# Fused attention and gated MLP: heads 0 to 7 of the output projection move into the MLP pass, weight splits move behind q and k, and twelve row maxima move into the prologue

## Chip, cores and metric

The kernel runs on one core of a Trainium2 chip. The metric is device time in microseconds (us) for one execution. Of the kernel before, three timed runs gave a median of 1876.55 us (1875.42 to 1880.77). One more execution was taken by the hardware profiler; every row quoted below is from that one.

## The reference, cut to what is computed

```
xn = layernorm(x)                       # x: 2048 x 512
q, k, v = xn @ wqkv                     # 32 heads of 16
attention = softmax(q k^T / 4) v, heads side by side, @ wo
z  = gelu(xn @ w_in)                    # 2048 x 1792
z1 = z[:, :896];  z2 = layernorm(z[:, 896:])
g  = w_sp @ z2 + b_sp                   # mixes the 2048 rows
out = x + attention + (z1 * g) @ w_out
```

All inputs are float32. The output is 2048 x 512.

## The kernel before: how the work is laid out

The kernel body runs once, as Python, and emits a fixed list of instructions for each engine. It has two parts: a **prologue** (lines 1005 to 1048) whose order is that of the code, and a **main loop** (lines 1264 to 1302) in which a small planner chooses the next TensorE (PE) instruction at each step. The planner keeps an estimated clock for each engine (`T`) and books its own cost for each operation. Nothing of it runs on the chip. On the chip each engine executes its list in order and waits on semaphores where data or buffers are not ready.

Precise products are made of three matmuls of parts ("hi" and "lo" halves of a float32, `split`, `mm3`, `dense`). A weight is split on GpSimd (POOL): a copy (L286) and a subtraction (L288), in `weight`. A split weight can be stored to DRAM (`ahead_of_time`) and fetched again later without POOL (`fetch_parts`).

**Attention** is done for 16 pairs of heads. For each pair and each of four chunks of 512 queries the loop makes:

- 16 *maxima* slots (`maxima`, L1128): two matmuls (L1136) into one PSUM slot and one VectorE (DVE) reduction of 128 x 1024 (L839 in `max_red`). After the 16th, `max_fin` reduces and transposes the result, stores it (`mscr`), and two DMAs from `mscr` write the maximum into the last rows of `qst`.
- 16 *score* slots (`scores`, L1122): two matmuls into a PSUM slot and one ScalarE (ACT) exponential (L74). A chunk's scores may start only when `maxready` says that its row has arrived. Before the first score the loop makes maxima only (from planner time `FIRST` = 7 on, up to `LEAD` = 30 of them) and dense slots.
- two *value* bursts (`values`, L1219): 32 matmuls each. There are 128 bursts, and the text calls the stretch from one burst to the next a **round**. `ORDER` lists a round's slots: S scores, M maxima, D dense, V the burst.

The PSUM slots are three tiles `sl` and one tile `dps` of two banks each. In the main loop `dps` belongs to the **dense** slots (L1181): two matmuls that run side by side on the upper and the lower 64 rows of the array. The dense work is a queue of generators (L1059): v of the later rows, q and k of the later heads, the z2 half of the MLP, its z1 half, the spatial mix, the MLP's output product (`mlp_out`), the attention's output product (`attn_out`). A generator yields slots in *pieces* of about 24 (`"q"` ends a piece) and evacuates `dps` at the end of an accumulation (`"e"`). After a piece ends, `hold` keeps the next one back until the next burst. So the queue advances one piece in a round. When no dense slot can be had, `filler` (L1195) may issue two dummy matmuls.

Buffers of 512 KB (`piece`, a ring of 19) are counted in `room["big"]`; generators and loaders wait on this count, and 256 KB buffers `t512` (4) are counted in `room["t5"]`.

Places that the change touches:

- Prologue: for each group g of 512 rows, `qk_first(g)` makes q and k of the first heads, `load_stacks` brings them into `qst` and `kst` through DRAM, `turn_x` and `norm_x` prepare the next group, and `v_tile` makes the first four v tiles. Their accumulators are taken in turn from (`dps`, `sl0`, `sl1`, `sl2`) by `bank()`.
- L1053: seven z1 weight splits (`w1`) are started at the head of the main loop. `wsp`, the 16 weights of the spatial mix's first 512 columns, are split at L631, when z1's last but one piece begins.
- `z2_all` (L557): before its last piece it waits until `room["big"] > 5`, and fetches group 0 of the normalized input for z1. `z1_all` follows.
- `spatial` (L681): waits until all four `t512` are free (L685), loads two z1 tiles, and then works through 28 units of 48 slots, two pieces each.
- `norm_out` (L863): normalizes the attention output of eight heads of one chunk: two POOL products, a split and a store to `oscr`. It waits for the one `ogrp` buffer.
- `mlp_out` (L777): 16 pieces of 21 slots (7 blocks of `w_out`, three matmul pairs each). `attn_out` (L926): 8 pieces of 24 slots (4 blocks of `wo`), each followed by the addition `fin` (L929); it waits for the heads of the last group but one (`lasthl`). The last pair of heads is added at the end by `last_pair` (L962), `last_norm`, `last_mm` (L977) and `last_add` (L984), which wait for the `fin` additions.

## Time and profile before

| what | value |
|---|---|
| timed runs, median | 1876.55 us |
| the profiled execution, its own time | 1873.65 us |
| its span, first to last instruction | 1871.9 us |
| mean granted TensorE clock | 0.994 |
| first dense slot of the main loop | 64.07 us |
| first score matmul | 105.20 us |
| first value burst, last value burst (start) | 119.2 us, 1845.1 us |
| GpSimd busy | 721.0 us (39%) |
| ScalarE busy | 1188.7 us (64%) |

The span is one execution seen by the profiler; what lies around it is 1.75 us. Its own time is 2.9 us below the median of the timed runs, so a sum made against the profile is carried over to the median as a difference. In rows of a timeline the columns are start, duration, engine, line, operation, output<-inputs, form and count; a bracket gives the idle time before and what ended it. In rows of a table by windows, each pair is busy time and count.

### The profile page before, as it was taken

How to read it: one execution, taken by the hardware profiler on the slowest of the kernel's cores; microseconds unless marked ns; L12 is line 12 of the kernel's file. 1: busy time of each engine (PE TensorE's matmuls, PEld its weight loads, DVE VectorE, ACT ScalarE, POOL GpSimd, SP SyncE). 2: the span in 40 equal slices, each digit the busy share in tenths (PEclk: the TensorE clock that was granted, in tenths of full speed). 3: DMA queues.
4: the chain of work that ended last, by engine and by line, in shares of the span. 5: the costliest groups of instructions: out<-in, count | busy, mean ns of one | idle time of the engine just before them, and what ended most of it. 6: DMA issues, size and time to landing. Idle time of an engine off the chain costs nothing.

```text
span 1871.9 us, 38101 instructions
## 1 busy us (share of the span) xinstructions
PE 1821.7 (97%) x14848; PEld 1103.6 (59%) x14848; DVE 1443.5 (77%) x1677; ACT 1188.7 (64%) x1292; POOL 721.0 (39%) x808
## 2 busy tenths in 40 slices
PE   6989999999999999999999999999999999999998
PEld 5756566655654565466666656565655656555555
DVE  6568878888897887878787878777877878788863
ACT  2147777687676677766666666566656666666653
POOL 5412242778879768710145203400352222002110
PEclk9999999999999999999999999999999999999999
DMA  7836572533566343366568665744766757475544
GB/s 230 295 121 190 193 238 87 126 91 109 135 225 192 117 125 98 88 152 150 153 196 194 175 170 164 177 129 128 186 189 163 185 155 181 119 150 158 154 132 142
DMA packets 209309, 297.75 MB, mean 159 GB/s; under 512 B 36049, under 2 KB 107281, under 8 KB 206241
## 3 DMA queue, kind: packets, MB, share of 16 engines
q1 hardware_dynamic: 200008, 265.44, 51.8%
q0 software_dynamic: 9120, 29.89, 4.9%
q8 instruction: 116, 1.90, 0.4%
q14 instruction: 65, 0.52, 0.1%
HBM read 189.60 MB, written 105.65 MB: 158 GB/s over the span
## 4 chain that ended last, share of the span: by engine, by line
PE 85%; DVE 5%; POOL 4%; issue 2%; DMA 2%; ACT 1%; SPq 0%; DVEq 0%; POOLq 0%; ACTq 0%
PE dps L1181 33%; PE sl L1219 23%; PE sl L1122 14%; PE sl L1136 12%; DVE mm L839 4%; PE dps L1195 1%; POOL wsp L288 1%; ACT pf L74 1%; POOL wsp L286 1%; DMA zs<-z2scr 0%; PE sl L242 0%; PE sl L241 0%; PE sl L240 0%; POOL z2hl L542 0%; DMA kscr<-qkhl 0%
## 5 line engine op out<-in xcount | busy, mean ns | idle before, releaser
L839 DVE TENSOR_REDUCE mm<-sl 128x2 f32<-128x1024 f32 x1024 | 1224.2, 1222 | 209.2 <-PE sl L1136 204.7
L74 ACT ACTIVATE pf<-sl 128x1024 f32<-128x1024 f32 x1024 | 1041.1, 1026 | 337.3 <-PE sl L1122 300.1
L1219 PE MATMUL sl<-pf,vall 128*32 128x512 f32 x4096 | 467.3, 597 | 0.0
L1122 PE MATMUL sl<-qst,kst 50*128 50x512 f32 x2048 | 443.3, 422 | 14.0 <-DVE mm L839 5.1
L1181 PE MATMUL dps<-wsp,zs 64*128 64x512 f32 x2688 | 439.4, 393 | 2.7 <-DMA zs<-z2scr 2.7
L1136 PE MATMUL sl<-kst,qst 48*128 48x512 f32 x2048 | 427.1, 407 | 3.4 <-DVE mm L839 1.8
L1122 PEld LDWEIGHTS sl<-qst,kst 50*128 50x128 f32 x2048 | 197.7, 184 | 225.5 <-issue 84.0
L1181 PEld LDWEIGHTS dps<-wsp,zs 64*128 64x128 f32 x2688 | 265.0, 187 | 44.8 <-DMA zs<-z2scr 4.7
L1219 PEld LDWEIGHTS sl<-pf,vall 128*32 128x32 f32 x4096 | 120.3, 110 | 268.3 <-issue 236.1
L1136 PEld LDWEIGHTS sl<-kst,qst 48*128 48x128 f32 x2048 | 198.1, 185 | 109.6 <-ACT pf L74 57.6
L747 POOL TENSOR_TENSOR hhl<-z1i,hhl 128x512 fp32r<-128x512 f32 x28 | 35.6, 1284 | 371.4 <-ACT hhl L74 371.4
L74 ACT ACTIVATE e<-sl 128x512 f32<-128x512 f32 x64 | 38.2, 598 | 212.6 <-PE sl L1219 194.2
L1239 DVE TENSOR_TENSOR e<-sl,e 128x512 f32<-128x512 f32 x64 | 44.3, 692 | 132.3 <-PE sl L1219 68.9
L1181 PE MATMUL dps<-w,xt 64*128 64x448 f32 x768 | 110.8, 368 | 1.5
L1181 PE MATMUL dps<-wout,hp 64*128 64x512 f32 x672 | 109.6, 392 | 0.0
L882 POOL TENSOR_TENSOR ob<-ob 128x512 f32<-128x512 f32 (+1 forms) x16 | 20.5, 1282 | 193.6 <-DMA ob<-escr 193.6
L1181 PEld LDWEIGHTS dps<-w,xt 64*128 64x128 f32 x768 | 73.7, 186 | 16.1 <-issue 7.8
L438 POOL TENSOR_TENSOR qkhl<-qr,qkhl 128x512 fp32r<-128x512 f32 x24 | 30.4, 1283 | 129.5 <-ACT qkhl L74 93.3
L886 POOL TENSOR_TENSOR ob<-ob 128x512 f32<-128x512 f32 (+1 forms) x16 | 20.5, 1283 | 147.1 <-DMA ob<-rscr 147.1
L1181 PEld LDWEIGHTS dps<-wout,hp 64*128 64x128 f32 x672 | 65.2, 187 | 9.4
L1195 PE MATMUL dps<-brow,zeror 64*128 64x512 f32 x276 | 51.8, 399 | 0.5 <-DVE fin L929 0.3
L1181 PE MATMUL dps<-xnT,wqk 64*128 64x512 f32 x288 | 47.4, 396 | 1.1 <-ACT vall L74 0.4
(285 smaller groups left out, 1617.9 us busy)
## 6 DMA issues: line engine op xcount, KB each, us to landing
zs<-z2scr SPq DMA_DIRECT2D x192, 256.0 KB
escr<-e SPq DMA_DIRECT2D x60, 256.0 KB
hscr<-hhl POOLq DMA_DIRECT2D x28, 512.0 KB, 6.0
qst<-qscr SPq DMA_DIRECT2D x30, 384.0 KB
kst<-kscr SPq DMA_DIRECT2D x30, 384.0 KB
qscr<-qkhl SPq DMA_DIRECT2D x16, 512.0 KB
kscr<-qkhl SPq DMA_DIRECT2D x16, 512.0 KB
xscr<-xnT POOLq DMA_DIRECT2D x16, 512.0 KB, 6.7
```

What stands on the lines that cost most here:

```text
L74: return nc.scalar.activation(out, in_, func, **kw)
L438: nc.gpsimd.tensor_sub(hl[:, 1, :], raw_, hl[:, 0, :].bitcast(F32))
L747: nc.gpsimd.tensor_sub(hl[:, 1, :], z1, hl[:, 0, :].bitcast(F32))
L839: nc.vector.tensor_reduce(mmax[g][:, :, t, kc], sl[k], AX.X, ALU.max)
L882: nc.gpsimd.tensor_add(both_[rows, 0, :], both_[rows, 0, :], both_[rows, 1, :])
L886: nc.gpsimd.tensor_mul(both_[rows, 0, :], both_[rows, 0, :], both_[rows, 1, :])
L1122: nc.tensor.matmul(sl[k][:, j, :], kst[p % 2][rows, kt * P:(kt + 1) * P], qst[p % 2][rows, c * 512:(c + 1) * 512], start=True, stop=True)
L1136: nc.tensor.matmul(sl[k][:, j, :], qst[p % 2][rows, tt * P:(tt + 1) * P], kst[p % 2][rows, kc * 512:(kc + 1) * 512], start=True, stop=True)
L1181: nc.tensor.matmul(dps[:, bank, :w], lhs, rhs, start=go, stop=stop)
L1195: nc.tensor.matmul(dps[:, bank, :], zeror[r:r + 64], brow[r:r + 64], start=not begun, stop=not begun)
L1219: nc.tensor.matmul(sl[k][cols:cols + VW, 0, :], vpack(kt + r, 2 * p + j), pf[:, j * 512:(j + 1) * 512], start=n == n_pv, stop=n == n_pv + ...
L1239: nc.vector.tensor_add(e, sl[k][:, 0, :], e)
```

## The change

It does these things:

1. `first_maxima` makes 12 of the 16 maxima of the first chunk in the prologue: four after the v tiles of group 2, eight after those of group 3. Their accumulators come from the same rotation of four tiles. The main loop starts with `n_mx` = 12, and the first 16 maxima are taken column block by column block.
2. The seven `w1` splits start with `qk_rest` instead of the head of the main loop. Eight of the 16 first `wsp` weights are split there too, four in group 3 and four in group 0, and stored to DRAM (`wsscr`); later they are fetched.
3. `z2_all` no longer waits for room before its last piece: a task (`fetch_first`) fetches group 0, and `z1_all` waits for it.
4. `spatial` no longer waits for the `t512` buffers before its first unit: a task (`first_z1`) loads the z1 tiles, and the evacuation waits for them.
5. Block 0 of `wo` (heads 0 to 7) is used in `mlp_out`, whose pieces have 24 slots; `attn_out` keeps three blocks and pieces of 18. `norm_out` of heads 0 to 7 waits until the spatial mix has used eight parts of z2.
6. `attn_out`'s addition waits for a value burst; `hold` acts only when all v tiles are done.

```diff
+QUART = 3
+KEPT = 8
+OUTS = 8
...
+    def first_maxima(kc):
+
+        for t in range(4):
+            turns[0] += 1
+            acc = (dps, *sl)[turns[0] % 4]
+            for j in range(2):
+                rows = slice(64 * j, 64 * j + KS)
+                nc.tensor.matmul(acc[:, j, :], qst[0][rows, t * P:(t + 1) * P], kst[0][rows, kc * 512:(kc + 1) * 512], start=True, stop=True)
+            if 0 not in mmax:
+                mmax[0] = at_.tile([P, 2, 4, 4], F32, tag="mm", name="mm0", bufs=2)
+            nc.vector.tensor_reduce(mmax[0][:, :, t, kc], acc, AX.X, ALU.max)
...
     def qk_rest():
+        for f in range(NF):
+            owed[0] += 1
+            spawn(ahead_of_time(f, (f"w1_{f}", w_in[:, f * P:(f + 1) * P], D, ND), w1scr[f], AHEAD), 1)
...
+                if (g, m) in ((3, 1), (0, 1)):
+                    for s in range(KEPT // 2) if g else range(KEPT // 2, KEPT):
+                        owed[0] += 1
+                        spawn(ahead_of_time(s, sp_weights(0, s), wsscr[s], AHEAD), 1)
...
+    def fetch_first():
+        for c in range(ND):
+            yield "C", lambda: room["big"] > 2
+            xnT[0, c] = piece(f"xnT0_{c}_")
+            move(xnT[0, c], xscr[0][c])
+        fetched[0] = True
+        late1[0] = 1
...
             if t == NT - 1:
-                yield from need(lambda: room["big"] > 5)
-                fetch_xnT(0)
-                late1[0] = 1
+                spawn(fetch_first(), 1)
...
     def z1_all():
+        yield from need(lambda: fetched[0])
...
-                    prepare(wsp, [((0, s), *sp_weights(0, s)) for s in range(NT)], spare=kept)
+                    for s in range(KEPT):
+                        spawn(fetch_parts(wsp, (0, s), wsscr[s], kept), 1)
+                    prepare(wsp, [((0, s), *sp_weights(0, s)) for s in range(KEPT, NT)], spare=kept)
...
+    def first_z1(g, fs):
+        yield "C", lambda: room["t5"] > 3
+        for f in fs:
+            load_z1(g, f)
...
-            if n == 0:
-                yield from need(lambda: room["t5"] > 3)
             if opens:
-                for f in {x, y}:
-                    load_z1(g, f)
+                if n:
+                    for f in {x, y}:
+                        load_z1(g, f)
+                else:
+                    spawn(first_z1(g, (x, y)), 1)
...
+            yield from need(lambda: (g, x) in z1s and (g, y) in z1s)
...
+                if i:
+                    move(h[r, :, n * P:], oscr[r, :, 0, u * P:(u + 1) * P])
...
-                for f in range(NF):
+                for f in range(NF + 1):
...
-        g, (t, kc) = i // 16, divmod(i % 16, 4)
+        g, (t, kc) = i // 16, divmod(i % 16, 4) if i >= 16 else (i % 4, i // 4)
...
-        yield open_("ogrp")
+        yield "C", lambda: room["ogrp"] > 0 and (g4 or zused[0] > OUTS)
...
         def out_(t):
+            yield "C", lambda: mode == "V" or n_pv == N
...
-                yield from dense(4, lambda g: ops(g, False), lambda g: ops(g, True), (q, 1 - q), not q, q == 1)
+                yield from dense(3, lambda g: ops(g + 1, False), lambda g: ops(g + 1, True), (q, 1 - q), not q, q == 1)
...
             for t in ((), (0,), (1, 2), (3,))[g]:
                 v_tile(t, wv)
+            if 2 <= g <= QUART:
+                first_maxima(g - 2)
+            if g == 3 and QUART == 3:
+                first_maxima(2)
...
-        for f in range(NF):
-            owed[0] += 1
-            spawn(ahead_of_time(f, (f"w1_{f}", w_in[:, f * P:(f + 1) * P], D, ND), w1scr[f], AHEAD), 1)
...
-        n_st = n_mx = n_pv = 0
+        n_st, n_mx, n_pv = 0, 4 * QUART, 0
...
-                    hold = spent > 11 and n_pv < N
+                    hold = spent > 11 and n_pv < N and len(vdone) == NT - EARLY
```

Left out of the diff: the DRAM tiles, the eighth block (`wo0`) in the list of the MLP's weights and its counts, the three blocks left in `attn_out`'s list, and the order of the first 16 maxima in `maxima`, which is that of `max_red`.

More of the change, by code (lines that the diff above doesn't have):

```diff
@@ L114, in fused_block @@
     mscr = [dr.tile([4, 32, 32], F32, name=f"mscr{i}") for i in range(4)]
+    wsscr = [dr.tile([P, 2, 512], F32, name=f"wsscr{s}") for s in range(KEPT)]
     w1scr = [dr.tile([P, 2, 512], F32, name=f"w1scr{f}") for f in range(NF)]
@@ L303, in fetch_parts @@
         yield "C", lambda: room["big"] > 1 + spare[0]
-        t = piece(f"wf{k}")
+        t = piece(f"wf{len(out)}_{len(wsp)}")
         move(t, scr)
@@ L695, in spatial @@
                 else:
-                    prepare(wout, [(f, f"wout{f}", w_out[f * P:(f + 1) * P, :], 512) for f in range(NF)], spare=(2,))
+                    prepare(wout, [(f, f"wout{f}", w_out[f * P:(f + 1) * P, :], 512) for f in range(NF)] + [(NF, "wo0", wo[0:P, :], 512)], spare=(2,))
             if not opens:
@@ L794, in mlp_out @@
                 selectors()
-                prepare(wo_, [(g, f"wo{g}", wo[g * P:(g + 1) * P, :], 512) for g in range(4)], spare=(-9,))
+                prepare(wo_, [(g, f"wo{g}", wo[g * P:(g + 1) * P, :], 512) for g in range(1, 4)], spare=(-9,))
             for q in range(2):
@@ L807, in mlp_out @@
                     ops = lambda _: (h[:, 0, c], h[:, 1, c], wout[f][:, 0, :], wout[f][:, 1, :])
-                    yield from dense(1, ops, ops, (q, 1 - q), not q and f == 0, q == 1 and f == NF - 1)
+                    yield from dense(1, ops, ops, (q, 1 - q), not q and f == 0, q == 1 and f == NF)
                 lease("big", 2)
@@ L931, in out_ @@
             added[t] = ends[0]
-        yield from need(lambda: len(wo_) == 4)
+        yield from need(lambda: len(wo_) == 3)
         for t in range(0, NT, 2):
```

11 lines of the change are left out of this document (6 added, 5 removed).

## The prediction

> **What bounds the kernel now.** I read the page's engine rows first, then the shares of the chain that ended last, and then a table by windows, one window for each round.
>
> ```profile
> span 1871.9 us, 38101 instructions
> PE 1821.7 (97%) x14848; PEld 1103.6 (59%) x14848; DVE 1443.5 (77%) x1677; ACT 1188.7 (64%) x1292; POOL 721.0 (39%) x808
> ...
> PE 85%; DVE 5%; POOL 4%; issue 2%; DMA 2%; ACT 1%; SPq 0%; DVEq 0%; POOLq 0%; ACTq 0%
> ```
>
> PE is 97% busy and carries 85% of the chain. That looks like a kernel with nothing to win except less matmul work, and this change removes none. The next rows say otherwise. They count the matmuls of dense slots (two to a slot) around the passage from z1 to the spatial mix; behind them stand rows of all engines for one round without dense work and two with it.
>
> ```profile
> 755.90:768.20 12.30, 0.00 (x0) 0.00 (x0) 1.00 0.58 153
> 768.20:781.50 13.30, 0.00 (x0) 0.00 (x0) 1.00 0.12 41
> 781.50:794.10 12.60, 0.00 (x0) 0.00 (x0) 1.00 0.07 23
> ...
> 755.90:768.20 12.30, 12.01 (x84) 5.04 (x82) 10.79 (x12) 8.56 (x10) 11.20 (x14) 1.00 0.58 153
> 861.10:874.10 13.00, 13.00 (x116) 7.95 (x117) 9.82 (x11) 7.68 (x8) 0.00 (x0) 1.00 0.32 84
> 874.10:887.70 13.60, 13.60 (x120) 8.21 (x118) 10.62 (x13) 9.18 (x9) 0.00 (x0) 1.00 0.81 162
> ```
>
> A round with 24 dense slots takes 13.0 or 13.6 us; one with none takes 12.3 to 13.3. So a round costs nearly the same whether a dense piece rides in it or not. Busy PE time hides this: the empty round still reads 12.01 busy of 12.30, while weight loading (the second pair) falls from 7.95 to 5.04.
>
> The time is therefore 128 rounds, plus the stretch ahead of the first burst, plus the stretch behind the last. Three rounds are empty here. The other place is from z2 to z1:
>
> ```profile
> 507.10:520.00 12.90, 0.00 (x0) 0.00 (x0) 1.00 0.41 111
> 520.00:533.90 13.90, 0.54 (x4) 0.38 (x4) 1.00 0.50 155
> ...
> 561.20:574.60 13.40, 4.93 (x30) 2.79 (x30) 1.00 0.80 243
> ...
> 590.10:605.10 15.00, 1.95 (x14) 1.14 (x12) 0.86 0.71 211
> ...
> 590.10:605.10 15.00, 12.38 (x76) 5.08 (x74) 9.40 (x10) 8.87 (x11) 14.56 (x17) 0.86 0.71 211
> ```
>
> These four rounds lack 24, 22, 9 and 17 slots, three pieces in all. The last of them is also 2.0 us longer than a full round of 13.0, and POOL works 14.56 of its 15.00 us (the last row, where the fifth pair is POOL). What was delayed comes out behind the last burst:
>
> ```profile
> 1833.00:1845.10 12.10, 7.13 (x50) 4.76 (x48) 1.00 0.62 184
> 1845.10:1871.90 26.80, 12.10 (x96) 8.77 (x96) 0.98 0.23 85
> ...
> 1850.31 2.34 PE L1181 MATMUL dps<-wo,op 64*128 64x512 f32 x18
> ...
> 1857.76 2.35 PE L1181 MATMUL dps<-wo,op 64*128 64x512 f32 x18 [1.33 <-DVE fin L929]
> ...
> 1863.84 1.14 PE L977 MATMUL sl<-sel,on 32*128 32x512 f32 x8
> ...
> 1853.17 0.29 DVE L970 TENSOR_TENSOR on<-sl,on 128x128 f32<-128x128 f32 x1
> ```
>
> Two whole pieces (96 matmuls) run after the last burst, from 1850.31 on: 13.5 us with one wait of 1.33 for an addition, so 6.1 for a piece of 24 and 4.6 for one of 18. The nine slots (x18) of the first row start about 0.24 apart, which is a slot's price below. The last pair's factor is ready at 1853.46 (L970), but its product (L977) waits for them until 1863.84: **10.4 us** of tail that two recovered pieces would remove.
>
> **The change, part by part. The opening.** First the end of the prologue, then the way to the first score.
>
> ```profile
> 55.06 0.39 PE L240 MATMUL sl<-xnT,wqk 128*128 128x512 f32 x1
> 64.07 1.69 PE L1181 MATMUL dps<-qst,xnT 64*128 64x512 f32 x12 [0.69 <-ACT vall L74]
> ...
> 70.53 10.52 DVE L839 TENSOR_REDUCE mm<-sl 128x2 f32<-128x1024 f32 x9 [8.46 <-PE sl L1136]
> ...
> 105.20 0.99 PE L1122 MATMUL sl<-qst,kst 50*128 50x512 f32 x2 [2.56 <-DMA qst<-mscr]
> ...
> 64.00:105.10 41.10, 32.09 (x226) 21.81 (x226) 1.00 0.74 259
> ...
> 105.20:109.40 4.20, 4.20 (x19) 3.16 (x21) 1.04 (x1) 1.21 (x2) 0.26 (x1) 0.59 0.99 332
> 119.20:134.00 14.80, 14.28 (x118) 8.97 (x116) 10.44 (x9) 9.57 (x11) 0.00 (x0) 1.00 0.02 3
> ```
>
> Nine reductions in a row take 10.52 us, 1.17 each. The four new maxima of group 2 stand in front of the matmul at 55.06 and push the following ones by about 1.6 us (four slots of 0.24, and 0.6 for an accumulator still being reduced). PE's prologue ended at 63.38 (64.07 less the idle 0.69). So the eight of group 3 begin near 65.0, and their reductions run to about 65.5 + 8 x 1.17 = 74.9. The rotation of four tiles, counted through, puts the last of them into `dps`, the tile of the first dense slot. So the main loop starts at 75.0 instead of 64.07: **PE nearly idle for some 9 us**, 10.9 us later.
>
> In return 12 reductions go from the main loop, 12 x 1.17 = 14.0 us. PE came to the first score at 102.64 (105.20 less the idle 2.56), 38.6 after the first dense slot; now 24.6. The idle 2.56 ahead of the score was followed by 4.2 us at a granted clock of 0.59, a loss of 1.7; I charge that once to the new idle stretch. First score: 75.0 + 24.6 + 1.7 = 101.3.
>
> The wait of 2.56 should go as well, because SP, which issues every load and store here in order, is rid of seven loads and seven stores of the z1 weights:
>
> ```profile
> 91.25 0.21 DVE L856 STREAM_TRANSPOSE ms<-mrow 128x32 f32<-128x32 f32 x1
> ...
> 95.35 0.74 SPq L129 DMA_DIRECT2D w1scr<-w  x1
> ...
> 97.92 0.69 SPq L129 DMA_DIRECT2D mscr<-ms  x1
> ```
>
> The row was ready at 91.46 and its store left at 97.92, behind stores that waited for POOL. After the change the row is ready near 91.46 - 64.07 - 14.0 + 1.7 + 75.0 = 90.1 and needs 105.20 - 97.92 = 7.3 us: 97.4, ahead of 101.3.
>
> First burst: 14.0 us behind the first score, as before, less the lost 1.7: 113.6 (before 119.2). But 14.0 us at 113 slots in 41.1 us are 39 slots less of v, and the second burst needs all 144. With 74 + 27 slots at the first burst, 43 remain, where the second round held 28: 15 extra x 0.24 + 1 for an evacuation = 4.6. Second burst: 113.6 + 14.8 + 4.6 = 133.0, against 134.0. **The opening gains 1.0 us and falls one dense piece behind.**
>
> On the idle clock the Trainium skill ("TensorE: Matmul & The Clock Gate", sections "What's actually happening" and "Why this matters for your kernels") speaks against this edit: an idle window of about 3.4 us halves the clock until about 3.4 us of work have passed, and gaps up to about 3 us are harmless. By it, as an estimate, the 2.56 us before the change cost no clock and the new idle stretch would cost 1.7 us: the opening would lose 0.7 instead of gaining 1.0. The row with 0.59 disagrees on the short gap.
>
> **Splits moved to q and k.** A split weight costs POOL a copy and a subtraction, 1.90 us; 15 of them (seven from the opening, eight from z1's end) stand now in this stage:
>
> ```profile
> L286 POOL CAST wsp<-wsp_0r 128x512 fp32r<-128x512 f32 x4 | 2.5, 613 | 16.2 <-PE sl L1136 13.3 <-PE dps L1181 2.9
> L288 POOL TENSOR_TENSOR wsp<-wsp_0r,wsp 128x512 fp32r<-128x512 f32 x4 | 5.1, 1287 | 0.3
> ...
> 149.50:284.80 135.30, 134.46 (x1122) 81.35 (x1120) 107.43 (x119) 100.38 (x116) 39.42 (x37) 1.00 0.64 207
> ```
>
> 15 x 1.90 = 28.5 us on top of POOL's 39.42 of 135.30: room enough, and I cost it at nothing. Its 15 loads and 15 stores pass SP there; if SP is held by POOL as at 97.92, the price is 6.5 us on one maximum row.
>
> **z2 to z1.** The last z2 piece no longer waits for six free buffers, and `norm_out` of heads 0 to 7 leaves this POOL-bound stretch:
>
> ```profile
> L882 POOL TENSOR_TENSOR ob<-ob 128x512 f32<-128x512 f32 (+1 forms) x16 | 20.5, 1282 | 193.6 <-DMA ob<-escr 193.6
> ```
>
> Its four POOL steps (the product, one like it, a split of 1.9) come to 4.5 us a chunk, 18 for four; they go to the spatial stage, where POOL reads 0.00 in the two rounds quoted first, and cost nothing there unless they meet the splits of the next 512 columns. Between none and three pieces come back; I take **two**, because POOL still has z2's and z1's own work. The round of 15.00 may lose its 2.0; against it z1 now starts right behind its loads, six of 512 KB at once, where before a round lay between. I set these two against each other, at nothing.
>
> **z1 to spatial.** The first unit waited for z1's last gelu to free the `t512` buffers: its last product ended at 793.4 and the dense rows resume at 794.1.
>
> ```profile
> 792.09 1.28 POOL L611 TENSOR_TENSOR z<-z 128x512 f32<-128x512 f32 x1
> ```
>
> That wait goes, and 8 x 1.9 = 15 us of splits, which stood ahead of that gelu, go too. What is late next: the last of the 16 weights, whose buffers z1 still holds by the code (`kept`). The new wait for the z1 tiles stands four rounds later, at an evacuation, with only dense slots queued behind it; I cost it at nothing. Again none to three pieces, I take **two**. Two rounds that fill up grow from a mean of 12.7 to one of 13.3: +1.1.
>
> **MLP and projection.** MLP pieces grow from 21 to 24 slots:
>
> ```profile
> 1578.60:1592.40 13.80, 13.75 (x118) 7.80 (x120) 11.24 (x15) 9.08 (x9) 0.00 (x0) 1.00 0.58 163
> 1592.40:1605.30 12.90, 12.55 (x106) 7.63 (x104) 10.17 (x10) 7.78 (x8) 0.00 (x0) 1.00 0.33 75
> ```
>
> They take 13.80 and 12.90 with 21 slots (x42); the spatial rounds took 13.6 and 13.0 with 24. So 48 slots move into free room at no cost. SP gets 32 more loads there, under DMA that is busy 0.58 and 0.33 of the time; hidden. The projection's addition, which now waits for a burst, holds back only its own queue, which `hold` keeps until that burst anyway. If that room isn't there, each of 16 rounds grows by three slots of 0.24: +11.5. The last three rounds have no maxima left (12.10 with 24 slots) and are bound by PE; with 18 slots each loses 6 x 0.24: **-4.3**.
>
> **Sum.** Pieces: -1 + 2 + 2 = 3 ahead, so none is left for the tail: -10.2 (10.4 less a short gap). Opening -1.0, passages +1.1, last rounds -4.3: **-14.4**. Against the profiled execution, 1873.65 (span 1871.9 and 1.75 around it), that is 1859.3; the median stands 2.9 higher, which gives **1862**. Pieces of 18 make it robust: with one piece left behind (4.6 and 1.3) the tail still gains 7, with two 3. The lower bound has all six pieces back: the last three rounds then carry none and lose up to 18 x 0.24 each, 13 in all: 1849.
>
> **Rivals.** The third rests on three rows: the reductions done before the first score, the arrival of the second chunk's row, and the first score that uses it.
>
> ```profile
> L839 DVE TENSOR_REDUCE mm<-sl x26: 1184/1222/1227, 70.5 to 101.7; 128x2 f32<-128x1024 f32 x26
> ...
> 121.78 1.28 SPq L129 DMA_DIRECT2D qst<-mscr  x2
> ...
> 137.58 0.50 PE L1122 MATMUL sl<-qst,kst 50*128 50x512 f32 x2
> ```
>
> 1. *Room decides the passages, not POOL and not the waits removed.* No piece comes back, the opening's one is added, and three stand behind the last burst: 3 x 4.6 + 2 x 1.3 against 13.5 makes the tail 2.9 longer. -1.0 - 4.3 + 2.9 = -2.4: 1874. For it: the code waits for buffers in both places, and the change adds none. Against it: at the second place the row of 792.09 stands right ahead of the restart, so it was that wait. The change would then not do what it says. Chance 0.12.
> 2. *MLP rounds are PE-bound.* +11.5 - 14.4 = -2.9: 1874. Against it stand the equal rows above. Chance 0.12; both of these together +9.1, 1886, chance 0.04.
> 3. *Slower: the lead of the maxima shrinks.* Before, 26 reductions are done at the first score, ten of them for the next chunk. If the shorter opening leaves fewer, each chunk's row comes later, and a stalled score doesn't let the planner catch up, so every chunk pays. Chunk 1 has 13.2 us in hand (its row lands about 2.6 behind the issue of 121.78, scores from 137.58); a missing maximum costs 13.3 / 8 = 1.7. It decides from eight missing on; at nine each of 63 chunks loses 2: some +110, far beyond 1900. By the reckoning above the planner makes as many between row and score as before, since that stretch has not changed. Chance 0.08.
>
> **How the numbers follow.** The forecast holds 0.64: 0.58 from 1850 to 1868 and 0.06 below. About 0.3% (5.6 us) is what a measurement of this kernel can tell from no change, so faster means under 1871. The forecast's 0.64 and 0.08 of rivals 1 and 2 are faster, 0.72; the other 0.16 of these two is the same; rival 3 and the pair, 0.12, are slower. The range 1850 to 1876 leaves out 0.12 above and 0.06 below.
>
> **What would show it.** First dense slot near 75, reductions of L839 in the prologue, half clock behind them; first score near 101, second burst near 133 with v only just done. Fewer empty rounds between z2 and the spatial mix. MLP rounds of 24 slots at 13.0 and 13.7. L977 at the end about 5 us behind the last burst. Wrong would be: empty rounds at the same places, or scores that wait for `qst<-mscr` in every chunk.

## The result and the profile after

The changed kernel takes **1890.51 us** (median of 5 runs, 1885.88 to 1893.36) against 1875.42 for the kernel before (5 runs, 1872.23 to 1880.77): the ratio is **1.0074, 95% interval 1.0054 to 1.0094**. It is 0.7% slower, where 0.8% faster was forecast. The profiled execution of after has a span of 1888.7 us, 16.8 more than before.

The page of after, its engine rows and the chain that ended last:

```profile
span 1888.7 us, 38013 instructions
PE 1819.1 (96%) x14752; PEld 1102.0 (58%) x14752; DVE 1440.8 (76%) x1677; ACT 1192.6 (63%) x1292; POOL 722.2 (38%) x808
...
PE 82%; DVE 6%; DMA 4%; POOL 4%; issue 2%; ACT 1%; SPq 0%; DVEq 0%; POOLq 0%; ACTq 0%
```

The engines do nearly the same work as before: PE issues 96 matmuls fewer, all of them dummies of `filler` (276 before, 180 after), and the DMA moves 306 MB where it moved 298. The chain differs more: DMA has 4% of it where it had 2%. So hardly anything was added; something waits. To see where, I cut both executions at the starts of the same bursts (round n runs from the n-th burst to the next). All numbers are differences of burst starts, in us, good to 0.1:

| stretch | before | after | difference |
|---|---|---|---|
| start to round 10 | 243.9 | 242.7 | -1.2 |
| round 10 | 13.8 | 19.9 | **+6.1** |
| rounds 11 to 30 | 276.1 | 277.6 | +1.5 |
| rounds 31 to 40 (z2 to z1) | 140.6 | 154.6 | **+14.0** |
| rounds 41 to 60 (z1 to spatial) | 266.5 | 269.3 | +2.8 |
| rounds 61 to 94 | 464.1 | 468.2 | **+4.1** |
| rounds 95 to 124 | 403.1 | 403.4 | +0.3 |
| rounds 125 to 127 | 36.9 | 36.0 | -0.9 |
| behind the last burst | 26.8 | 17.0 | -9.8 |

First what answers to the forecast's steps. The opening, in a timeline of VectorE, PE and SyncE's queue; then a table by windows of the dense matmuls alone (two to a slot; first pair PE, second weight loading) and one of all engines (PE, weight loading, DVE, ACT, POOL, granted clock, DMA share, GB/s):

```profile
74.68 1.22 DVE L418 TENSOR_REDUCE mm<-dps 128x2 f32<-128x1024 f32 x1
75.95 2.93 PE L1226 MATMUL dps<-qst,xnT 64*128 64x512 f32 x12 [3.73 <-DVE mm L418]
91.10 0.34 SPq L133 DMA_DIRECT2D mscr<-ms  x1
101.22 0.40 PE L1167 MATMUL sl<-qst,kst 50*128 50x512 f32 x2
```

```profile
540.20:554.50 14.30, 3.92 (x24) 2.19 (x24) 1.00 0.96 335
554.50:568.80 14.30, 4.08 (x26) 2.42 (x24) 1.00 0.63 198
...
776.40:789.30 12.90, 3.62 (x24) 2.28 (x24) 1.00 0.45 128
789.30:802.80 13.50, 3.79 (x24) 2.29 (x24) 1.00 0.67 178
```

```profile
1606.20:1620.00 13.80, 13.80 (x116) 7.96 (x114) 10.63 (x13) 9.19 (x9) 0.00 (x0) 1.00 0.24 59
1620.00:1633.00 13.00, 13.00 (x116) 7.96 (x118) 11.02 (x11) 7.67 (x8) 0.00 (x0) 1.00 0.82 211
...
1871.70:1888.70 17.00, 10.31 (x94) 4.59 (x94) 6.89 (x8) 1.79 (x2) 0.00 (x0) 0.93 0.34 125
```

First dense slot 75.95 (forecast 75.0), row stored at once at 91.10, first score 101.22 (101.3), first and second burst 113.94 and 134.0 (113.6 and 133.0). At the passages half pieces ride where whole ones were missing. MLP rounds hold 24 slots in 13.8 and 13.0 us. No dense slot is left behind the last burst, and the tail is 9.8 us shorter (10.2). Most of what the change was priced for, it does; the second burst and the last three rounds fall short of the forecast. Then where rounds became long:

```profile
242.70:262.60 19.90, 15.63 (x116) 9.80 (x114) 11.13 (x14) 10.91 (x13) 2.53 (x2) 0.91 0.89 269
540.20:694.80 154.60, 145.21 (x1110) 84.23 (x1109) 111.19 (x130) 96.97 (x110) 116.35 (x138) 0.96 0.51 150
1152.30:1187.10 34.80, 30.38 (x234) 18.00 (x232) 21.89 (x27) 17.41 (x18) 26.65 (x29) 0.95 0.82 203
1387.90:1405.50 17.60, 15.49 (x120) 10.06 (x122) 10.73 (x14) 9.22 (x9) 4.48 (x4) 0.90 0.57 149
```

The first two of these stretches before the change:

```profile
243.90:257.70 13.80, 13.72 (x116) 8.18 (x114) 10.98 (x14) 10.65 (x13) 7.18 (x9) 1.00 0.78 269
533.90:674.50 140.60, 135.65 (x1080) 77.67 (x1078) 113.81 (x132) 95.67 (x108) 109.98 (x127) 0.98 0.56 171
```

In each of the four stretches after the change PE is idle for some time (length less the first pair) and the granted clock, the number after the POOL pair, falls below 1. In **round 10** the row of maxima came late. A timeline of SyncE's queue and PE, then a window of all engines behind the wait:

```profile
230.41 0.39 SPq L133 DMA_DIRECT2D mscr<-ms  x1
...
234.05 0.38 SPq L133 DMA_DIRECT2D wsscr<-wsp  x1
...
238.61 2.29 SPq L133 DMA_DIRECT2D kscr<-qkhl  x2
243.07 1.68 SPq L133 DMA_DIRECT2D qst<-mscr  x2
...
250.55 0.84 PE L1167 MATMUL sl<-qst,kst 50*128 50x512 f32 x2 [4.18 <-DMA qst<-mscr]
```

```profile
250.50:254.90 4.40, 4.35 (x23) 3.36 (x25) 1.76 (x2) 2.05 (x2) 0.00 (x0) 0.61 1.02 196
```

The row was stored at 230.41, but its way back left SyncE only at 243.07, behind stores of split weights (`wsscr`) that waited for GpSimd and the loads and stores of q and k queued behind them. PE waited 4.18 us and then worked 4.4 us at a clock of 0.61, a loss of 1.7: together 5.9 of the 6.1. In **round 33** three engines are coupled. A timeline of GpSimd, ScalarE and PE, then a window behind the wait:

```profile
573.07 1.01 POOL L567 TENSOR_TENSOR z2hl<-z,z2hl 128x384 fp32r<-128x384 f32 x1
574.05 1.25 POOL L637 TENSOR_TENSOR z1u<-z1u,z1x 128x512 f32<-128x512 f32 x1
...
575.34 0.63 ACT L77 ACTIVATE z1u<-z1u 128x512 f32<-128x512 f32 x1 [6.63 <-POOL z1u L637]
...
576.50 0.80 PE L1167 MATMUL sl<-qst,kst 50*128 50x512 f32 x2 [2.46 <-ACT e L77]
```

```profile
576.50:582.80 6.30, 6.28 (x28) 4.34 (x28) 2.67 (x3) 3.93 (x4) 3.52 (x4) 0.52 0.66 202
```

GpSimd still normalizes z2 (L567) between the steps of z1's first gelu (L637). ScalarE has z1's tanh at the head of its list and waits 6.63 us; the evacuation and the exponentials stand behind it, and PE behind those: 2.46 idle, and 3.0 more on a clock of 0.52 (6.3 x 0.48). That is the 5.5 by which this round exceeds a normal one of 13.4. The Trainium skill ("PSUM — Partial Sum Buffer", section "Engine vs sequencer instructions") calls the queues of ScalarE, VectorE and GpSimd strictly first in, first out; the row of 575.34 agrees.

### The profile page after: what moved, and what is told of

Read it like the earlier page. It is cut to its first block, busy times and chain, and to the rows that moved or that the text cites. A ratio compares the mean times of both kernels' runs of the same rounds, so it can differ in the third digit from the quotient of the medians.

```text
span 1888.7 us, 38013 instructions
## 1 busy us (share of the span) xinstructions
PE 1819.1 (96%) x14752; PEld 1102.0 (58%) x14752; DVE 1440.8 (76%) x1677; ACT 1192.6 (63%) x1292; POOL 722.2 (38%) x808
## 4 chain that ended last, share of the span: by engine, by line
PE 82%; DVE 6%; DMA 4%; POOL 4%; issue 2%; ACT 1%; SPq 0%; DVEq 0%; POOLq 0%; ACTq 0%
PE dps L1226 33%; PE sl L1264 22%; PE sl L1167 13%; PE sl L1181 11%; DVE mm L882 4%; POOL wsp L292 1%; ACT pf L77 1%; PE dps L1240 1%; DMA zs<-z2scr 1%; DMA qst<-mscr 1%; DMA mscr<-ms 1%; DVE mm L418 1%; DMA wsscr<-wsp 0%; POOL wsp L290 0%; PE sl L246 0%
## 5 line engine op out<-in xcount | busy, mean ns | idle before, releaser
L882 DVE TENSOR_REDUCE mm<-sl 128x2 f32<-128x1024 f32 x1012 | 1211.4, 1223 | 205.7 <-PE sl L1181 202.6
L1226 PE MATMUL dps<-wsp,zs 64*128 64x512 f32 x2352 | 389.3, 394 | 4.3 <-DMA zs<-z2scr 4.3
L1226 PEld LDWEIGHTS dps<-wsp,zs 64*128 64x128 f32 x2352 | 235.0, 188 | 39.4 <-DMA zs<-z2scr 3.8
L1226 PE MATMUL dps<-wf,zs 64*128 64x512 f32 x336 | 54.3, 392 | 0.0
```

The source lines that it names most:

```text
L882: nc.vector.tensor_reduce(mmax[g][:, :, t, kc], sl[k], AX.X, ALU.max)
L1226: nc.tensor.matmul(dps[:, bank, :w], lhs, rhs, start=go, stop=stop)
```

## Experiments

Theory: the pieces come back as forecast, but each moved step lands where a list executed in order (SyncE's, ScalarE's behind GpSimd's) has no slack, and PE pays the wait and a slow clock. Rivals: the rounds merely shift, so that undoing one part moves the long round elsewhere; or buffers and loads, not the order of waits, make them long. Ratios are to the kernel before with 95% intervals; the edits are to the changed kernel unless said otherwise.

### z2 to z1: three runs

**The old wait** before the last z2 piece put back.

```
-                spawn(fetch_first(), 1)
+                yield from need(lambda: room["big"] > 5)
+                fetch_xnT(0)
+                late1[0] = 1
...
-        yield from need(lambda: fetched[0])
```

> The changed kernel, but the last z2 piece waits for six free buffers again and group 0 is fetched there, as in the kernel before. Theory (z1 started on top of z2's normalization, whose POOL backlog blocks ScalarE and so PE): the rounds 31 to 41 take 138 us in all, as they did before, instead of 154.6, and two rounds become empty again, two pieces of 4.6 and a gap of 1.3 each later in the tail. Net -16 + 12 = 4 us faster: 1886. Rival A (pieces decide, long rounds move elsewhere): 12 us slower, 1902. Rival B (the early start costs nothing, the long rounds come from the norm_out work or another source): rounds 31 to 41 stay above 150 us and the time is 1890 to 1902.

1865.69 us, ratio **0.9947 (0.9932 to 0.9961)**. One part undone turns 0.7% slower into 0.5% faster. Windows of all engines, round 30, rounds 31 to 40, rounds 125 to 127:

```profile
526.30:539.70 13.40, 13.17 (x96) 6.00 (x94) 12.89 (x20) 11.24 (x12) 9.98 (x20) 1.00 0.22 70
539.70:677.80 138.10, 135.69 (x1102) 80.39 (x1100) 109.85 (x129) 96.54 (x109) 108.42 (x129) 1.00 0.56 161
...
1814.10:1848.10 34.00, 32.78 (x292) 18.59 (x292) 10.74 (x16) 23.89 (x27) 4.12 (x4) 1.00 0.31 101
```

Rounds 31 to 40 fall from 154.6 to 138.1, at a clock of 1.00, for one empty round (30). No piece reaches the tail for it, so the gain was 24.4 us of span where the theory had 4: the two pieces that I charged were not missed. Rounds 61 to 94 are 5.7 shorter too (462.5 against 468.2).

**GpSimd's gelu steps left out** for half of z1.

```
         yield "G", 1.05
-        nc.gpsimd.tensor_mul(u, x, x)
+        if g > 1:
+            nc.gpsimd.tensor_mul(u, x, x)
```

and so on for the five steps; tanh reads `x`.

> The changed kernel with GpSimd's five elementwise steps of z1's gelu left out for the first two of the four groups of rows (ScalarE's tanh and the store stay, and the planner keeps booking the steps' cost, so the order on every engine is the same). Theory (in rounds 31 to 40 GpSimd is behind its plan, tanh waits for it at the head of ScalarE's queue, and the exponentials and PE behind that): ScalarE's waits of 6.63 and 4.75 us for GpSimd vanish, rounds 31 to 40 fall from 154.6 to 138 to 144 us, time 1876 to 1881; round 10 stays at 19.9. Rival (the z1 loads, 3 MB at once, or the buffers hold these rounds): 150 us or more, time 1886 to 1891.

1882.35 us, ratio 1.0047 (1.0034 to 1.006), between the theory's time and the rival's. ScalarE's tanh of round 33 in a timeline of this run, with no wait ahead of it:

```profile
566.70 0.62 ACT L77 ACTIVATE z1u<-z1x 128x512 f32<-128x512 f32 x1
```

Windows of this run for round 33 and for rounds 36 to 40, and the latter in the changed kernel:

```profile
566.90:580.40 13.50, 13.22 (x112) 8.10 (x111) 11.67 (x13) 8.09 (x9) 3.69 (x4) 1.00 0.86 248
...
607.50:685.80 78.30, 74.29 (x564) 43.54 (x563) 54.99 (x64) 49.82 (x58) 5.84 (x6) 0.96 0.35 105
```

```profile
616.50:694.80 78.30, 74.33 (x567) 43.48 (x567) 54.98 (x64) 50.14 (x58) 50.86 (x54) 0.96 0.36 106
```

Round 33 falls from 19.0 to 13.5, as the theory said. Rounds 36 to 40 do not move: 78.3 us with GpSimd at 5.84 and with it at 50.86. There GpSimd is not the cause, and half of my theory for this stretch falls. These rounds hold 15, 27, 27, 27 and 24 dense slots: the pieces no longer begin with the rounds, and an evacuation of `dps` stands in the middle of each (two rows of PE in the changed kernel):

```profile
654.01 0.51 PE L1167 MATMUL sl<-qst,kst 50*128 50x512 f32 x2 [0.41 <-DVE mm L882]
655.23 0.96 PE L1226 MATMUL dps<-xnT__6213,wf 64*128 64x512 f32 x6 [0.49 <-ACT z1x L77]
```

With the old wait the same five rounds take 69.0 us with 24 slots each. So 7.3 of the 16.5 us between the two are GpSimd's (154.6 - 147.3, rounds 31 to 40). The other 9 go along with the way the pieces lie against the bursts; that this is their cause is argued, not shown, for no run changed it alone. In the changed kernel PE's waits in these five rounds are all short and add up to 3.9 us (0.7 with the old wait), and two stretches of half clock of 3.4 us each stand among them (none with the old wait), a loss of 3.4 more. Which of the short waits costs most was not isolated.

**A wait for GpSimd instead of buffers.**

```
-        yield from need(lambda: fetched[0])
+        yield from need(lambda: fetched[0] and normed[0] >= NT - 1)
```

(`normed` counts z2 tiles that are done.)

> The changed kernel with one more condition: z1 starts only when all but the last of the 16 z2 tiles have passed their GpSimd normalization in the plan (not when buffers are free). Theory (the wait for six buffers was in effect a wait for GpSimd, and that is what it was worth): one round near 30 empty, rounds 31 to 40 at 138 to 142 us instead of 154.6, time 1866 to 1872, near the 1865.7 of the run with the old wait. Rival (buffers and the loads of z1 are what matters, 3 MB at once): rounds 31 to 40 stay above 148 us and the time is 1880 to 1891.

1871.12 us, ratio 0.9975 (0.9966 to 0.9984). Rounds 31 to 40 take 135.6 us (from 540.9 to 676.5), so waiting for GpSimd cures them as well. Three of these ten rounds carry no dense work here, but the full rounds 36 to 40 are cured too: 68.9 us with 24 slots each. Their pieces begin with the rounds again, so this run does not separate the two causes. And it waits longer than needed: with three empty rounds two pieces stand in the tail again (23.8 us). The theory's time held, its one empty round did not.

### Weights behind q and k: three runs

**None moved.**

```
-KEPT = 8
+KEPT = 0
```

> The changed kernel, but all 16 spatial weights of the first 512 columns are split at the end of z1 again, as in the kernel before (none behind q and k). Theory (the loss is where moved work meets a queue that executes in order): round 10, where the scores waited 4.18 us for their row behind four stores of split weights and then ran on a low clock, falls from 19.9 to 13.8 us; start of round 11 comes 6.0 us earlier. The 15 us of splits at the end of z1 cost up to one piece again (one empty round, 5.9 in the tail). Time 1884.5 if no piece is lost, 1890 if one is. Rival (the row was late because of the z1 weight splits or because all rounds stand elsewhere): round 10 or a neighbour stays above 18 us, time 1890 to 1896.

1885.1 us, ratio 1.0054 (1.0042 to 1.0066). The window of round 10, and the row's way in a timeline of SyncE and PE:

```profile
242.60:256.40 13.80, 13.71 (x118) 8.09 (x116) 11.00 (x14) 10.71 (x13) 2.53 (x2) 1.00 0.48 179
```

```profile
229.63 0.34 SPq L133 DMA_DIRECT2D mscr<-ms  x1
236.18 1.79 SPq L133 DMA_DIRECT2D qst<-mscr  x2
...
246.18 0.50 PE L1167 MATMUL sl<-qst,kst 50*128 50x512 f32 x2
```

The row's loads leave 6.6 us behind its store, not 12.7, and PE does not wait. The stall was that of the moved weights, and it did not turn up elsewhere.

**None moved, and the old z2 wait** (both edits).

> The changed kernel with two parts undone: the last z2 piece waits for six free buffers again, and all 16 first spatial weights are split at the end of z1 again. Theory (the two losses are separate, each at its place): round 10 falls from 20.3 (in the run with the z2 wait alone) to 13.8, and the rest stays as in that run, so 1865.7 - 6.5 = 1859, a ratio of 0.992 to the kernel before; up to 1863 if the 15 us of splits cost a part of a piece at the end of z1. Rival (the rounds merely shift, a stalled row turns up elsewhere): 1864 to 1870 with some other round above 18 us.

1866.69 us, ratio 0.996 (0.9947 to 0.9972): the forecast missed. The time is the rival's, though no round reaches its 18 us. Round 10 is 13.8, but rounds 47 to 53 cost 3.9 us more than with eight weights moved (96.8 against 92.9), rounds 64, 78 and 92 are 15.5 to 15.8, and 18 slots stand in the tail. Eight weights moved are worth about what round 10 costs.

**Four moved**, at the first place only, and the old z2 wait.

```
-KEPT = 8
+KEPT = 4
...
-                if (g, m) in ((3, 1), (0, 1)):
-                    for s in range(KEPT // 2) if g else range(KEPT // 2, KEPT):
+                if (g, m) == (3, 1):
+                    for s in range(KEPT):
```

> The changed kernel with the z2 wait of before and only four spatial weights split behind q and k, those of the first of the two places (rounds 3 to 8, where the changed kernel's rounds were not longer); the other twelve at the end of z1. Theory (it is the second place, whose stores meet the loads of the next heads and the maximum row of round 10, that costs): round 10 is 13.8, time 1858 to 1861, as with all 16 at the end or a little less. Rival (any stores of split weights in that stage delay a row): some round from 4 to 12 above 16 us, time 1862 to 1866.

1862.53 us, ratio **0.9932 (0.9919 to 0.9945)**, as fast as any run here, though 1.5 us above the theory's range. Round 10 and rounds 31 to 40:

```profile
242.90:256.60 13.70, 13.62 (x116) 8.13 (x114) 10.91 (x14) 10.67 (x13) 2.53 (x2) 1.00 0.53 202
...
533.40:671.40 138.00, 135.60 (x1102) 80.33 (x1100) 109.96 (x129) 96.51 (x109) 108.47 (x129) 1.00 0.55 162
```

It was the second place alone that met the maximum row.

### The opening: three runs

**z1's splits at the head of the loop again**, the changed kernel otherwise.

```
     def qk_rest():
-        for f in range(NF):
-            owed[0] += 1
-            spawn(ahead_of_time(f, (f"w1_{f}", ...), w1scr[f], AHEAD), 1)
```

(the same lines stand ahead of the loop again).

> The changed kernel, but the seven z1 weight splits start at the head of the main loop again. Theory: the store of the first maximum row waits again behind stores of split weights, as before (it left 6.5 us after the row was ready); the first burst comes some 2 to 6 us later than 113.9, and round 10 stays near 19.9 because the spatial weights are still split there; time 1892 to 1897. Rival (the z1 splits are what crowds round 10): round 10 falls to 13.8, time 1885 to 1890.

1888.32 us, ratio 1.0071 (1.0058 to 1.0084), no difference. Round 10 stays at 19.8; but the first burst comes at 113.3, not later: with the maxima of the prologue the row is no longer held (its store leaves at 90.41). This half of the theory was wrong.

**No maxima in the prologue**, on the run with both parts undone.

```
-QUART = 3
+QUART = 0
```

> As the run with both parts undone, but none of the first chunk's maxima are made in the prologue. The prediction's step (the opening gains 1 us, because the v tiles it does not make come after the first burst): 1 us slower than the run with both parts undone, with the first burst at 117 to 119 and the second near 134. Rival A (the whole lead of the first burst counts): 4 to 5 us slower. Rival B (the piece by which the opening falls behind counts): 3 to 5 us faster.

1862.37 us, ratio 0.9938 (0.9924 to 0.9952), 4.3 us faster than with them, as rival B had it. The row's store in a timeline of this run, its rounds 1 and 2 as windows, and those of the run with both parts undone:

```profile
91.92 0.34 SPq L133 DMA_DIRECT2D mscr<-ms  x1
```

```profile
115.00:129.80 14.80, 14.28 (x122) 8.94 (x121) 10.41 (x9) 9.58 (x11) 5.57 (x6) 1.00 0.48 152
129.80:145.30 15.50, 14.88 (x120) 8.68 (x118) 11.22 (x15) 9.40 (x11) 7.08 (x8) 1.00 0.50 165
```

```profile
114.20:134.40 20.20, 19.28 (x162) 12.66 (x163) 10.78 (x10) 10.55 (x13) 5.59 (x6) 1.00 0.15 41
134.40:148.20 13.80, 13.71 (x117) 8.00 (x115) 9.51 (x12) 9.32 (x11) 0.00 (x0) 1.00 0.25 99
```

Without them the row is stored at 91.92 (before 97.92), the first burst is at 115.0 (before 119.2, later by only 0.7 than with them), and the third comes at 145.3 against 148.2. So moving z1's splits alone gives 3 to 4 us at the first burst (the run with the MLP's part alone, below, has the opening of before and its first burst at 117.7), and the prologue's maxima take 2.9 of it back by the third: two remedies for one wait, and the dearer one on top.

**Four weights moved, old z2 wait, no maxima in the prologue.**

> The changed kernel with the z2 wait of before, only four spatial weights split behind q and k (at the first place), and no maxima in the prologue. Theory (the last two runs add up: half the weights moved is worth 4 us against none moved, and the prologue's maxima cost 3 us at the third burst): third burst at 145.3 instead of 148.1, time 1858 to 1860, a ratio of 0.992. Rival (the 4 us between the runs with and without the prologue's maxima came from where the pieces fell, not from the opening): 1862 to 1866 although the third burst comes 3 us earlier.

1862.09 us, ratio 0.9935 (0.9921 to 0.9948), as fast as with the maxima: the rival. The third burst is at 145.2, but rounds 6, 75 to 76 and 92 (16.0, 14.9, 18.3, 18.0 us) give the 3 us back. For the total, where the pieces fall counts as much as the opening.

### Spatial wait, MLP, normalization: three runs

**The spatial wait put back** on the run with four weights moved.

```
+            if n == 0:
+                yield from need(lambda: room["t5"] > 3)
             if opens:
-                if n:
-                    for f in {x, y}:
-                        load_z1(g, f)
-                else:
-                    spawn(first_z1(g, (x, y)), 1)
+                for f in {x, y}:
+                    load_z1(g, f)
```

> The run with four weights moved and the z2 wait of before, and in addition the spatial mix waits for all four 256 KB buffers before its first unit again. Theory (that wait and the splits ahead of z1's last gelu are what empties rounds 47 to 49): one to one and a half pieces are lost, 18 slots each behind the last burst: 4 to 7 us slower than 1862.5, so 1866 to 1869. Rival (the weights alone decide when the spatial mix starts): no difference, 1861 to 1864.

1866.11 us, ratio 0.9959 (0.9945 to 0.9973), 3.6 us slower by the medians. Rounds 47 to 49 are empty again (no dense matmul from 755.3 to 793.6), and 18 slots more stand in the tail. The forecast's step for this place holds.

**The MLP's part alone**, on the kernel before (`wo0` as the eighth block of the MLP, three blocks in the projection, its addition at a burst).

> The kernel before with nothing changed but the block of the projection moved into the MLP pass (24 slots and 18), and the addition held until a burst. The prediction's step alone: MLP rounds stay at 12.9 and 13.7 us with 24 slots, the last three rounds lose some 1 us each, the two pieces of the tail have 18 slots each and cost 3 us less: 6 to 7 us faster, ratio 0.9965. Rival (the 48 slots are paid in the MLP rounds, 0.24 each): 4 us slower, ratio 1.002.

1870.4 us, ratio 0.998 (0.9971 to 0.9989), 4.1 us faster where 6 to 7 were forecast. An MLP round, rounds 125 to 127 and the tail:

```profile
1567.50:1580.60 13.10, 12.96 (x112) 7.96 (x110) 10.04 (x10) 7.79 (x8) 0.00 (x0) 1.00 0.72 162
...
1811.60:1845.50 33.90, 32.71 (x292) 18.86 (x292) 10.70 (x16) 23.84 (x27) 4.13 (x4) 1.00 0.47 146
1845.50:1869.60 24.10, 17.59 (x150) 9.88 (x150) 9.26 (x10) 1.79 (x2) 0.00 (x0) 0.98 0.28 104
```

MLP rounds cost next to nothing more (rounds 95 to 124 are 1.4 us longer together); the last three fall from 36.9 to 33.9 and the tail from 26.8 to 24.1.

**`norm_out` of heads 0 to 7 at once.**

```
-        yield "C", lambda: room["ogrp"] > 0 and (g4 or zused[0] > OUTS)
+        yield open_("ogrp")
```

> The changed kernel, but the normalization of the attention output of heads 0 to 7 runs as soon as its data is there, not only after the spatial mix has begun. It puts four times 4.5 us of POOL work back into rounds 26 to 36. Theory (POOL's backlog sets the length of rounds 31 to 41): these rounds grow by 5 to 18 us, time 1896 to 1908, and rounds 75 and 76 stay near 17.4. Rival (POOL's backlog there is without effect, and the moved normalization is what meets the weight splits in rounds 75 and 76): rounds 31 to 41 unchanged, rounds 75 and 76 fall to 13.4, time 1882.

1886.97 us, ratio 1.0066 (1.0052 to 1.0081): no difference that this comparison shows, and both accounts were wrong. Rounds 31 to 40 are shorter, not longer (148.0), rounds 75 and 76 are normal, but round 63 takes 22.3 us, 77 17.2 and 91 18.5. What rounds 31 to 40 win (6.6 us), rounds 61 to 94 lose (475.0 us against 468.2). So this part is not the cause of the loss in all, but here the long rounds did shift, as the rival of the experiments has it.

### Rounds 75, 76 and 92: four runs, one point open

In this stretch long rounds stand at other places in nearly every run: 79 and 93 (15.2 and 17.2 us) before the change, 91 (18.1) with the old z2 wait, 78 and 92 (15.5 each) with four weights moved. In the changed kernel PE's longest waits there are 1.46 and 1.48 us for z2's tiles (rounds 75 and 76) and 2.11 us for the row of maxima (round 92, as in round 10).

**The later spatial weights loaded from GpSimd's queue** instead of SyncE's.

```
-        move(dst, src)
+        if nm[:3] == "wsp" and nm[3] != "0":
+            nc.gpsimd.dma_start(raw(dst), raw(src))
+        else:
+            move(dst, src)
```

> The changed kernel, but the raw spatial weights of the second to fourth 512 columns are loaded from GpSimd's queue (16 loads at each of three passages, some 0.7 us each on GpSimd) and not from SyncE's, where they wait for GpSimd with z2's tiles and the maximum row behind them. Theory (SyncE's order makes the long rounds 75, 76 and 92): these three fall to 13.2 to 14.5 us, time 8 to 12 us below the 1890 of the changed kernel, 1878 to 1882. Rival (GpSimd's splits and the loads themselves are too much for two rounds; 11 us more work on GpSimd makes it worse): the rounds stay at 17 or grow, weights come late, 1888 to 1896.

1906.88 us, ratio 1.0175 (1.0161 to 1.019); worse. A window of round 61 of this run, then ScalarE and PE in a timeline of it:

```profile
961.90:981.80 19.90, 15.36 (x114) 9.79 (x112) 11.88 (x15) 8.08 (x9) 18.86 (x24) 0.91 0.84 219
```

```profile
972.61 0.63 ACT L77 ACTIVATE hhl<-z1i 128x512 fp32r<-128x512 f32 x1 [5.45 <-POOL z1i L782]
...
974.20 0.50 PE L1184 MATMUL sl<-kst,qst 48*128 48x512 f32 x2 [4.54 <-ACT pf L77]
```

It is round 33 once more: with more work on GpSimd (18.86 of 19.90 us), ScalarE waits for it at the head of its list, and PE for ScalarE.

The same edit on the two fastest variants was as bad: 1880.29 us, ratio 1.0035 (1.0022 to 1.0048), and 1882.86 us, ratio 1.0046 (1.0032 to 1.006).

> The run with the z2 wait of before, four weights moved and no maxima in the prologue, with the spatial weights of the second to fourth 512 columns loaded from GpSimd's queue. Theory: its rounds 75, 76 and 92 (14.9, 18.3, 18.0) fall to about 13.5, 10 us less: 1852 to 1855, ratio 0.989. Rival: 1860 to 1868.

> The run with the z2 wait of before and four weights moved (maxima in the prologue kept), with the spatial weights of the second to fourth 512 columns loaded from GpSimd's queue. Its long rounds there are only 14.5, 15.5 and 15.5 us; theory: 4 us less, 1857 to 1860. Rival: 1862 to 1868.

**GpSimd's subtraction left out** of these weights.

```
+        if a[0][:3] != "wsp" or a[0][3] == "0":
             nc.gpsimd.tensor_sub(t[:, 1, :n], rw, ...)
...
-    ops = lambda _: (zt[:, 0, c], zt[:, 1, c], w[:, 0, :], w[:, 1, :])
+    ops = lambda _: (zt[:, 0, c], zt[:, 1, c], w[:, 0, :], w[:, 1 if g == 0 else 0, :])
```

> The changed kernel, but for the spatial weights of the second to fourth 512 columns GpSimd's subtraction (1.28 us, 16 at each of three passages) is left out; the products that would take the low half take the high half again, so the matmuls are as many, and the planner books the same costs, so the order is the same. Theory (GpSimd's splits stand ahead of what SyncE and ScalarE wait for): rounds 75, 76 and 92 fall from 17.5, 17.3 and 17.6 to 13.2 to 14.5 us, 10 us less, 1880. Rival (the loads and the DMA queues are it, GpSimd's time is not): the three stay above 16 us, 1886 to 1891.

1883.99 us, ratio 1.0036 (1.0016 to 1.0056). Rounds 75, 76 and 92:

```profile
1156.50:1169.70 13.20, 13.20 (x117) 8.25 (x115) 11.21 (x12) 8.08 (x9) 7.67 (x9) 1.00 0.99 254
1169.70:1189.80 20.10, 17.23 (x118) 10.68 (x116) 10.67 (x15) 9.21 (x9) 4.94 (x7) 0.83 0.63 178
1390.80:1404.50 13.70, 13.70 (x120) 8.25 (x119) 10.60 (x14) 9.20 (x9) 3.21 (x3) 1.00 0.61 161
```

Round 92 is cured (13.7 where it took 17.6), which points to GpSimd there. Round 75 is too, but 76 grew from 17.3 to 20.1: the two take 33.3 us together where they took 34.8, so their wait has mostly moved by a round. PE waits in round 76 for z2's tiles while GpSimd is busy for 4.94 of 20.10 us. The profiled execution took 1890.48 us, 6.5 above the median of this kernel, so the size of its round 76 says little. What holds these loads **stays open**.

## Why the prediction was wrong, point by point

- *The opening.* The first score and the first burst came when forecast, but the second burst, where the gain of 1.0 was to show, came at 134.03, as before (134.01): the first round took 20.1 us, not 19.4. The -1.2 by round 10 comes from the round behind it (13.8 for 15.5) and is no larger than the scatter: in the twelve profiled executions whose engine lists up to the third burst are those of after, that burst starts anywhere from 146.5 to 150.0, and in the two with the lists of before at 148.1 and 149.5. That -1.2 stands beside -1.0 is luck. The account was incomplete, too: either remedy alone frees the row. The third burst starts at 147.2 with the maxima alone (one run), at 145.1 to 145.3 with the moved splits alone (three runs), so on top of the splits the maxima are a loss of some 3.
- *Splits moved to q and k.* **The first step that failed**: "room enough, and I cost it at nothing". I named the price, 6.5 on one maximum row, and the condition, SyncE held by GpSimd, and set neither into the sum nor into a rival. It cost 6.1, once.
- *z2 to z1.* **The step that decided**: "I set these two against each other, at nothing". I counted the slots that come back and not the length of the rounds that they come back into. The old wait for buffers also kept z1 behind z2's work on GpSimd and let pieces begin with rounds. Without it rounds 31 to 40 cost 14.0 more than before; with it, 16.5 less than in the changed kernel, and no piece was missing at the end. Of the 16.5, 7.3 are shown to be GpSimd's.
- *z1 to spatial.* Pieces came back as said (24 slots missing instead of three pieces), and the wait's worth is shown by its return. The stretch grew by 2.8 where the filled rounds were priced at 1.1.
- *MLP and projection.* Nothing for the MLP rounds: right. The last three rounds were mis-sized: with 18 slots each they fell by 2.9 (36.9 to 34.0, run with the old wait), not 4.3, and in the changed kernel by 0.9, with 13, 5 and 18. The round with 5 slots takes 11.4 us, as those with 18 do in the run with the old wait (11.3 to 11.4), so slots are no longer its bound.
- *Rounds 61 to 94.* No term of the sum; `norm_out`, moved into them, was to cost nothing there. They grew by 4.1. With `norm_out` put back they took 475.0, longer still, so what lengthens them stays open.
- *Tail.* -9.8 for -10.2.
- *The rivals.* None was what happened: room did not decide, MLP rounds are not PE-bound, and no chunk's row was late for want of lead. The slower side that I gave 0.12 was missing its likeliest mechanism, a coupling of lists executed in order, although the row of 97.92 showed one.

Between the forecast of -14.4 and the measured +16.8 lie 31.2 us: 14.0 from z2 to z1, 6.1 in round 10, 4.1 in rounds 61 to 94, 3.4 in the last three rounds, and most of the rest in rounds 11 to 30 (1.5) and 41 to 60 (1.7 beyond the 1.1 priced). With the z2 wait put back and the second four of the moved weights returned, the time is 1862.5, near the forecast's 1862; against the kernel before in the same comparison that is 12.0 us faster, where 14.4 were forecast. It is no proof of the sum: it rests on other rounds that moved (rounds 61 to 94 are 3.7 us shorter than before in that run, the last rounds longer than forecast).

## What to carry to other kernels

A slot in a round that has room is free only if nothing it brings with it stands at the head of a list that another engine needs: for each step moved, write down the two lists it enters (the engine's and the DMA queue's) and who is next in each. A wait that looks like waste may be what keeps two stages from overlapping on a third engine, so before removing it, ask what else it orders. And price rounds, not only slots: one late row cost as much as one piece recovered.

## What the runs showed of the hardware

A stall of PE costs its length and then some clock, and the price does not follow the length. In the 18 traces of this case, behind the first burst, PE sat idle for 2.09 us or more 26 times (up to 6.23 us). Each time the granted clock was at a half for 3.4 or 6.8 us (once 10.2), beginning within 4.4 us of the end of the idle stretch; for idle stretches of 1.3 to 2.07 us this was so in 11 of 26. After 2.46 us (round 33) the granted clock was 0.52 for 6.3 us, a loss of 3.0; after 4.18 us (round 10) 0.61 for 4.4 us, a loss of 1.7. The wait of round 10 stands in eight of the traces, 3.8 to 4.6 us long: with 3.4 us of half clock at it (five traces) the round takes 19.4 to 20.3 us, with 6.8 (three) 21.0 to 21.5. The Trainium skill ("TensorE: Matmul & The Clock Gate", section "Why this matters for your kernels") advises against gaps above about 3 us; here a gap below that halved the clock, so I would price a stall of PE of 2.09 us or more here at its length and 1.7 to 3.4 us more (half of 3.4 or 6.8).
